# One Strassen pair for the down projections of the first two chunks, and a second layer norm moved into the gate/up blocks

## The chip, the cores and the metric

The kernel runs on one core of a Trainium2 chip. TensorE multiplies matrices into PSUM; VectorE (DVE), ScalarE (ACT) and GpSimd (POOL) work element by element; SyncE (SP) issues most DMA transfers, and each engine has its own instruction queue, worked off in order. The metric is the time of one execution on the device, in microseconds (us); lower is better. A profile is one such execution recorded instruction by instruction.

## What is computed

A transformer block over S = 2048 tokens of width 1024, in bf16:

```python
q, k, v = split(layernorm(x) @ wqkv)                 # 32 heads of 32
idx     = pos[:, None] - 2 * arange(8)[None, :]      # 8 earlier positions, dilation 2
attn    = softmax(where(idx >= 0, q . k[idx] / sqrt(32), -1e9))
h       = x + (attn . v[idx]) @ wo                   # wo: 1024 x 1024
g, u    = layernorm(h) @ w_gate, layernorm(h) @ w_up # 1024 x 3584 each
out     = h + (g * u) @ w_down                       # 3584 x 1024
```

## The kernel before

**Tiling.** The tokens are cut into four chunks of 512 (`TC`). For a chunk, the normalized activations lie transposed in a tile `lnT` (128 partitions x 8 x 512 columns; pool of three). A gate or up group is eight matmuls of 128x128 by 128x512 into one PSUM bank (`mm_group`, L409); the PSUM pool has eight banks, all of them under one tag. The product g*u of a chunk, transposed, is 28 cells of [128, 512], and the down projection contracts over those cells.

**Strassen.** Where the kernel says "pair", two halves of a matrix product are combined so that seven block products take the place of eight, on operands scaled and converted to f16, with sums and differences of blocks made on VectorE. The scales are powers of two from sums of absolute values: `Scale.add` (L553) takes them on ScalarE, one instruction with an accumulated sum and a short read of the accumulator, and `Scale.total` adds them over partitions with one matmul by ones.

**Order of the work on TensorE before.** The stages stand in the order in which the program calls them:

1. qkv of chunks 0 to 3, interleaved; output projection 0 with its norm (`wo_ln2(0)`, L519) lies amid the last qkv blocks;
2. `ffn1(0)` (L602): seven blocks of gate and up groups of chunk 0. ScalarE copies each bank out, VectorE multiplies g by u, and ScalarE takes the absolute sums of the gate weights (for chunk 1, in step 4, of the up weights and of its hidden cells);
3. `wo_ln2(1)`, then `ffn2(0)` (L640): chunk 0's down projection with plain matmuls, 2 halves x 28 cells x 4 row tiles = 224;
4. `ffn1(1)`, then chunk 1's down projection as a Strassen pair of its own: its four row tiles are split into two and two, `dprod` (L805) makes a product of one row tile by one block over 14 cells, and there are seven products for each of two row tiles. Output projections 2 and 3 (`wo_adds`, L846) lie between these products, with the sums and conversions as functions hung onto their groups;
5. the pair blocks: gate and up of chunks 2 and 3 as Strassen products (`pair_block`, L703), and the down projection of chunks 2 and 3 as one pair over four row tiles.

**Output projection and norm.** `wo_ln2` makes 8 groups (4 row tiles x 2 halves). VectorE adds each bank to the residual `hs[t]` (L534). When a row tile is whole, VectorE takes its statistics (L181, L182), ScalarE the inverse deviation (L185, L186), VectorE normalizes (L190), and SP issues a DMA transpose into `lnT2`. The next gate/up stage needs all four transposes of its `lnT2` at its first matmul.

**Attention** of a chunk is a generator of VectorE steps (2.3 us and less each) with loads and stores on POOL's queue. `Background` (L38 and on) slips one step of it, or of a norm, between two matmul groups: each group gives `GROUP_US` = 1.73 of credit times `bg.rate`, and each step, or `bg.spend`, uses some of it. `bg.finish(gen)` emits all that is left of a generator at once. This is done while the program is built, so that it sets the order of each engine's instructions and takes no time itself.

**Weights.** The list `stream` holds the weight blocks in the order of their use; `pump` (L161) issues the next loads on SP's queue into a pool `wpool` of seven buffers, and `retire` (L173) gives buffers back. A load waits, on SP, for the readers of the buffer it overwrites.

Of the kernel before, what the change touches and what calls it, by code (L numbers as in the profile page):

```python
# [18 lines left out]
D = 1024  # L19
# [59 lines left out]
def kernel(  # L79
# [41 lines left out]

    bg = Background()
# [13 lines left out]
    def stream_wd(c, hf):  # L136
        for b in range(4):
            stream.append((("wd", c, hf, b), wd_v[:, bass.ts(b, 7), bass.ts(hf, 512)], 7))

    NH = NF // 4  # L140
    for c in range(2):
        stream_wo(c)
        if c > 0:
            stream_wd(0, 0)
            stream_wd(0, 1)
        for b in range(7):
            stream.append((("wg", c, b), wg_v[:, :, bass.ts(b, 512)], KO))
            stream.append((("wu", c, b), wu_v[:, :, bass.ts(b, 512)], KO))
    def stream_down(name, e, hf, halves):
        for a in halves:  # L150
            stream.append((("dn", name, a), wd_e[e][:, bass.ts(a, 7), bass.ts(hf, 512)], 7))

    stream_down("21", 1, 0, (0, 1))
    stream_down("11", 0, 0, (0, 1))
    stream_wo(2)
    stream_down("12", 0, 1, (0,))
# [100 lines left out]
    class NormOnScalar(Norm1):  # L257

        def sums(self):
            room = small.tile([128, 4, 4], F32, tag="nroom", name=f"nroom{self.c}")  # L260
            self.s, self.nm, self.ss, self.nb = (room[:, i, :] for i in range(4))
            junk = lnp.tile([128, D], BF, tag="ln", name=f"njunk{self.c}")
            xs = xtiles[self.c]
            for t in range(4):
                nc.scalar.activation(junk[:], xs[t][:], ACTF.Copy, accum_out=self.s[:, t:t + 1])
                yield "later", GROUP_US
            nc.scalar.activation(self.nm, self.s, ACTF.Copy, scale=-1.0 / D)
            for t in range(4):
                nc.scalar.activation(junk[:], xs[t][:], ACTF.Square, bias=self.nm[:, t:t + 1],
                                     accum_out=self.ss[:, t:t + 1])  # L270
                yield "later", GROUP_US
# [4 lines left out]

        def rows(self):
            for t in range(4):
                ln = lnp.tile([128, D], BF, tag="ln", name=f"ln{self.c}_{t}")
                nc.scalar.activation(ln[:], xtiles[self.c][t][:], ACTF.Identity, bias=self.nb[:, t:t + 1],  # L280
                                     scale=self.rs4[:, t:t + 1])
                self.lns[t] = ln
                self.transpose(t)
                yield "later", GROUP_US
# [158 lines left out]

    def attention(c):
        qD, kD = qkv_in["q", c], qkv_in["k", c]
        lg = att.tile([128, W, SUB], F32, tag="lg", name=f"lg{c}")
        for wp in range(W // 2):
# [14 lines left out]
            yield 1.0  # L462
        if c == 0:
            nc.vector.tensor_tensor(lg[0:32, :, 0:16], lg[0:32, :, 0:16], mask[:], ALU.add)
# [54 lines left out]
    def wo_ln2(c):  # L519
# [8 lines left out]
        for t in range(4):  # L528
            for hf in range(2):
# [12 lines left out]
                bg.spend(0.7)  # L542
                bg.step(GROUP_US)
        norm(3)
        retire(2)
        return lnT, hs
# [35 lines left out]
    scale_gu, scale_d, scale_h = Scale("gu", 56), Scale("d", 56), Scale("h", 56)  # L582
    scale_h1 = Scale("h1", 28)

    def abs_sum(c, b, j):
        wt = wts["wg" if c == 0 else "wu", c, b]
        junk = lnp.tile([128, 2, 512], BF, tag="ln", name=f"junk{c}_{b}_{j}")
        scale_gu.add(28 * c + 4 * b + j, wt[:, bass.ts(j, 2), :], junk[:])

    def abs_sum_down(hf, b, j):  # L590
        junk = lnp.tile([128, 512], BF, tag="ln", name=f"junkd{hf}_{b}_{j}")
        scale_d.add(28 * hf + 7 * b + j, wts["wd", 0, hf, b][:, j, :], junk[:])
# [5 lines left out]
    def abs_sum_h1(f, ht):  # L598
        junk = lnp.tile([128, TC], BF, tag="ln", name=f"junke{f}")
        scale_h1.add(f, ht[:], junk[:])  # L600

    def ffn1(c, lnT, at={}):  # L602
        hT = []
        for b in range(7):
            if b == 5 and c + 1 < NCH:
                hss[c + 1] = load_x(c + 1, "h", nc.sync)
            for j in range(4):
                pg = psum.tile([128, TC], F32, tag="mm", name=f"pg{c}_{b}_{j}")
                mm_group(pg, wts["wg", c, b], j, lnT)
                gs = t1k.tile([128, TC], BF, tag="t1k", name=f"gs{c}_{b}_{j}")  # L610
                nc.scalar.copy(gs[:], pg[:])  # L611
                bg.step(GROUP_US)
                pu = psum.tile([128, TC], F32, tag="mm", name=f"pu{c}_{b}_{j}")
                mm_group(pu, wts["wu", c, b], j, lnT)
                us = t1k.tile([128, TC], BF, tag="t1k", name=f"us{c}_{b}_{j}")
                nc.scalar.copy(us[:], pu[:])  # L616
                nc.vector.tensor_tensor(gs[:], gs[:], us[:], ALU.mult)  # L617
                abs_sum(c, b, j)
                bg.spend(0.45)
                bg.step(GROUP_US)  # L620
                hT.append(gs)
                if (b, j) in at:
                    at[b, j]()
                f = len(hT) - 3
                if c == 1 and f >= 0:
                    abs_sum_h1(f, hT[f])
# [3 lines left out]
        if c == 1:  # L630
            for f in range(NF - 2, NF):
                abs_sum_h1(f, hT[f])
        return hT

    def ffn2_store(c, t, hf, acc, hs, lo=0, n=512):
        cols = bass.ds(hf * 512 + lo, n)
        nc.vector.tensor_tensor(hs[t][:, cols], acc[:], hs[t][:, cols], ALU.add)
        nc.sync.dma_start(outf[bass.ds(c * TC + t * 128, 128), cols], hs[t][:, cols])

    def ffn2(c, hf, hT, hs, between={}):  # L640
        acc = [psum.tile([128, 512], F32, tag="mm", name=f"acc{c}_{hf}_{t}") for t in range(4)]
        for b in range(4):
            for j in range(7):
                f = b * 7 + j
                for t in range(4):
                    nc.tensor.matmul(acc[t][:], lhsT=hT[f][:, bass.ts(t, 128)],  # L646
                                     rhs=wts["wd", c, hf, b][:, j, :],
                                     start=(f == 0), stop=(f == NF - 1))
                if c == 0:
                    abs_sum_down(hf, b, j)  # L650
                bg.step(0.86)
            retire()
            if b in between:
                between[b]()
        for t in range(4):
            ffn2_store(c, t, hf, acc[t], hs)
            bg.spend(0.7)


# [103 lines left out]
    start_attention(1)  # L763
    pump(pair_at)
# [3 lines left out]
    qkv(3, range(4), last=True)  # L768
    bg.finish(atts[0])
    bg.rate = 0.98  # L770
# [3 lines left out]
    lnT2, hs = nxt  # L774
    hT = ffn1(0, lnT2)
    bg.finish(atts[1])
    nxt = wo_ln2(1)
    for hf in range(2):
        ffn2(0, hf, hT, hs)
    lnT2, hs = nxt  # L780
# [37 lines left out]
    dn = {}  # L818

    def first_blocks():  # L820
        dn["11"] = [wts["dn", "11", a] for a in range(2)]
        dn["21"] = [wts["dn", "21", a] for a in range(2)]
        conv_down(dn["11"])

    hT = ffn1(1, lnT2, {0: scale_d.rows, 2: scale_d.total, (6, 1): first_blocks})
# [332 lines left out]
```

## Time and profile before

| What | us |
|---|---|
| median of 3 runs (lowest, highest) | 778.18 (777.26, 778.30) |
| the profiled execution: time | 777.01 |
| the profiled execution: span of the profile | 775.2 |
| `wo_ln2(0)` | 163.56 to 177.38 |
| `ffn1(0)` | 191.19 to 287.88 |
| `wo_ln2(1)` | 287.88 to 301.69 |
| `ffn2(0)` | 301.69 to 350.04 |
| `ffn1(1)` | 350.04 to 446.76 |
| chunk 1's down projection, projections 2 and 3 | 446.76 to 516.77 |
| pair blocks of chunks 2 and 3 | 516.77 to 687 |
| down projection of chunks 2 and 3 | 687 to 775 |

The stages are read off TensorE's timeline, by the first matmul of each. Busy time on an engine is the union of its instructions' durations. A duration can be longer than the distance to the next start, since neighbouring instructions on an engine overlap; where an engine is backed up, the distance between starts is what one more instruction costs. A releaser, written `<-`, is what ended a wait, as inferred from semaphores. Within a group line of the page, the fields are: line of the program, engine, operation, output<-input, shapes, count, busy us, mean ns of one, idle time just before.

### The profile page before, as it was taken

To read this page: it belongs to the slowest core of one execution; us is meant where nothing else is said; L and a number is where in the kernel's file an instruction comes from. 1 tells how busy PE (TensorE), PEld (TensorE's weight loads), DVE (VectorE), ACT (ScalarE), POOL (GpSimd) and SP (SyncE) were. 2 spreads that over 40 slices of the span, in tenths; PEclk is the share of its full clock that TensorE was granted. 3 is DMA by queue.
4 is the path that set the end of the run, shared out by engine and by line. 5 is a ranking of instruction groups with operands and counts; after the bars stand their busy time and mean duration, and the time that the engine had idled before them with its cause. 6 is when DMAs were issued, how large, how long until landed. Compare 5 with 4: busy or idle time off the path is not lost.

```text
span 775.2 us, 10420 instructions
## 1 busy us (share of the span) xinstructions
PE 769.3 (99%) x3691; PEld 353.5 (46%) x3691; DVE 605.3 (78%) x766; ACT 484.0 (62%) x1040; POOL 142.1 (18%) x152
## 2 busy tenths in 40 slices
PE   8999999999999999999999999999999999999998
PEld 6444444444444444444444444444444444444444
DVE  5639999999999989999979859985553444578863
ACT  4639564322866662965777899746677776788240
POOL 0000000200002000011000001008778687600000
PEclk9999999999999999999999999999999999999999
DMA  8998896997947964978445592644332423740001
GB/s 278 265 260 199 157 230 151 299 271 224 310 133 236 308 235 125 288 257 277 142 143 192 182 299 68 157 98 114 109 95 69 109 59 106 240 140 28 0 28 55
DMA packets 183716, 134.38 MB, mean 173 GB/s; under 512 B 81264, under 2 KB 176496, under 8 KB 181616
## 3 DMA queue, kind: packets, MB, share of 16 engines
q1 hardware_dynamic: 176912, 110.12, 50.9%
q0 software_dynamic: 3584, 22.02, 8.9%
q10 hardware_dynamic: 3168, 1.57, 0.8%
q8 instruction: 29, 0.48, 0.3%
q14 instruction: 23, 0.19, 0.1%
HBM read 104.86 MB, written 22.02 MB: 164 GB/s over the span
## 4 chain that ended last, share of the span: by engine, by line
PE 93%; DVE 3%; DMA 2%; ACT 1%; issue 0%; ACTq 0%; DVEq 0%
PE ps L411 20%; PE pg L411 12%; PE pu L411 12%; PE dx L807 6%; PE pz L700 6%; PE acc L646 6%; PE py L700 6%; PE px L700 6%; PE wo L532 4%; PE wo L852 4%; PE pv L700 3%; PE dy L807 3%; PE ex L807 2%; DMA lnT<-lnr 1%; DMA w_qkv<-in_A_wqkv_dram 1%; PE ps L372 1%
## 5 line engine op out<-in xcount | busy, mean ns | idle before, releaser
L411 PE MATMUL ps<-lnT,w_qkv 128*128 128x512 bf16 x736 | 159.5, 379 | 0.0
L411 PEld LDWEIGHTS <-w_qkv 128*128 128x128 bf16 x736 | 71.9, 98 | 86.2
L411 PE MATMUL pu<-lnT,w_wu 128*128 128x512 bf16 x448 | 105.8, 379 | 0.0
L411 PE MATMUL pg<-lnT,w_wg 128*128 128x512 bf16 x448 | 105.8, 379 | 0.0
L324 ACT CAST sg<-ps 128x512 bf16<-128x512 f32 x96 | 55.2, 585 | 52.3 <-PE ps L411 49.2
L451 DVE TENSOR_TENSOR prod<-qD,kD 128x4096 bf16<-128x4096 bf16 x32 | 72.4, 2285 | 12.8 <-DMA kD<-kd 12.7
L494 DVE TENSOR_TENSOR pv<-vD,at 128x4096 bf16<-128x4096 bf16 x32 | 72.5, 2285 | 0.3
L700 PEld LDWEIGHTS <-sw 128*128 128x128 f16 x448 | 43.8, 98 | 53.8 <-issue 1.2
L411 PEld LDWEIGHTS <-w_wu 128*128 128x128 bf16 x448 | 43.8, 98 | 52.9
L411 PEld LDWEIGHTS <-w_wg 128*128 128x128 bf16 x448 | 43.7, 98 | 52.8
L616 ACT CAST us<-pu 128x512 bf16<-128x512 f32 x56 | 33.0, 590 | 43.0 <-PE pu L411 41.8
L700 PE MATMUL px<-lnT,ws 128*128 128x512 bf16 x224 | 55.2, 379 | 0.0
L700 PEld LDWEIGHTS <-ws 128*128 128x128 f16 x336 | 32.9, 98 | 39.7
L506 POOL DMA_DIRECT2D od<-oD x4 | 2.2, 542 | 264.3 <-DVE oD L504 264.3
L646 PE MATMUL acc<-w_wd,gs 128*128 128x512 bf16 x224 | 48.5, 379 | 0.0
L681 POOL TENSOR_TENSOR sw<-ws 128x512 f16<-128x512 f16 x26 | 30.0, 1152 | 85.1 <-PE py L700 77.8
L611 ACT CAST gs<-pg 128x512 bf16<-128x512 f32 x56 | 32.6, 583 | 12.9 <-PE pg L411 10.6
L453 DVE TENSOR_TENSOR prod<-prod 128x4096 bf16<-128x4096 bf16 x16 | 36.6, 2289 | 0.4
L560 ACT ACTIVATE junkd<-w_wd 128x512 bf16<-128x512 bf16 x56 | 34.3, 613 | 0.0
L646 PEld LDWEIGHTS <-gs 128*128 128x128 bf16 x224 | 21.9, 98 | 26.4
L617 DVE TENSOR_TENSOR gs<-gs,us 128x512 bf16<-128x512 bf16 x56 | 23.5, 419 | 12.5 <-ACT us L616 12.5
L185 ACT ACTIVATE rs<-mv,eps 128x1 f32<-128x1 f32 (+1 forms) x21 | 6.2, 297 | 42.0 <-DVE mv L182 36.6
(321 smaller groups left out, 1391.5 us busy)
## 6 DMA issues: line engine op xcount, KB each, us to landing
w_wg<-in_B_w_gate_dram SPq DMA_DIRECT2D x14, 1024.0 KB, 6.7
w_wu<-in_B_w_up_dram SPq DMA_DIRECT2D x14, 1024.0 KB, 5.4
w_wd<-in_B_w_down_dram SPq DMA_DIRECT2D x8, 896.0 KB, 6.2
w_pair<-in_B_w_gate_dram SPq DMA_DIRECT2D x14, 512.0 KB, 4.0
w_pair<-in_B_w_up_dram SPq DMA_DIRECT2D x14, 512.0 KB, 5.2
w_wo<-in_A_wo_dram SPq DMA_DIRECT2D x6, 1024.0 KB, 6.2
w_qkv<-in_A_wqkv_dram SPq DMA_DIRECT2D x5, 1024.0 KB, 11.0
kd<-sg SPq DMA_DIRECT2D x32, 144.0 KB, 3.3
```

The lines of the kernel that those rows point to most:

```text
L324: nc.scalar.copy(sg[:, HB:HB + TC], ps[:])
L411: nc.tensor.matmul(ps[:], lhsT=wt[:, ko, bass.ts(j, 128)], rhs=rhs[:, ko, :], start=(ko == 0), stop=(ko == KO - 1))
L451: nc.vector.tensor_tensor(prod[:, j], qD[:], kD[:, :, o:o + SUB], ALU.mult)
L453: nc.vector.tensor_tensor(prod[:, :, 0:16], prod[:, :, 0:16], prod[:, :, 16:32], ALU.add)
L494: nc.vector.tensor_tensor(pv[:, j], vD[:, :, o:o + SUB], at[:, w, None, :].to_broadcast((128, DH, SUB)), ALU.mult)
L532: nc.tensor.matmul(ps[:], lhsT=oTs[c][:, kk, t, :], rhs=wts["wo", c, hf][:, kk, :], start=(kk == 0), stop=(kk == KO - 1))
L560: nc.scalar.activation(junk, src, ACTF.Abs, accum_out=self.l1[:, k:k + 1])
L611: nc.scalar.copy(gs[:], pg[:])
L616: nc.scalar.copy(us[:], pu[:])
L646: nc.tensor.matmul(acc[t][:], lhsT=hT[f][:, bass.ts(t, 128)], rhs=wts["wd", c, hf, b][:, j, :], start=(f == 0), stop=(f == NF - 1))
L700: nc.tensor.matmul(ps[:], lhsT=lhs[:, ko, :], rhs=rhs[:, ko, :], start=(fresh and ko == 0), stop=(ko == 3), skip_group_check=not fresh)
L807: nc.tensor.matmul(ps[:, bass.ds(lo, n)], lhsT=lhs[k][:, bass.ts(q, 128)], rhs=rhs[k][:, bass.ds(lo, n)], start=(fresh and k == 0), stop=( ...
```

## The change

**Chunk 0's plain down projection is gone.** `ffn2` is removed. Chunk 0's hidden cells stay in SBUF, chunk 1's are stored to DRAM (`hd1`) in pairs from a ring of small tiles, and reloaded. After both gate/up stages, chunks 0 and 1 are down-projected as one Strassen pair over four row tiles: 7 products x 4 row tiles x 14 cells.

**Output projection 1** moves from after `ffn1(0)` to before block 5 of chunk 0's gate/up (`ffn1_first`, called with `{5: wo_1}`). Its norm's row sums, squares and normalized rows are ScalarE activations (`Norm2`, a subclass of the norm that the qkv stage uses); the squares and rows are slipped into blocks 5 and 6 as a background generator.

**What goes with it.** Residual rows of chunks 0 and 1 are stored to DRAM (`hsd0`, `hsd1`) and reloaded into weight buffers. The absolute sums of w_down are taken earlier: blocks 0 to 2 are loaded on ScalarE's queue during qkv of chunks 2 and 3 (`abs_early`), blocks 3 to 7 during chunk 1's gate/up (`abs_gen`). Absolute sums of weights are 2048 wide instead of 1024 (gate and up) or 1024 instead of 512 (w_down). `bg.rate` goes from 0.98 to 1.0.

```diff
-    for c in range(2):
-        stream_wo(c)
-        if c > 0:
-            stream_wd(0, 0)
-            stream_wd(0, 1)
-        for b in range(7):
-            stream.append((("wg", c, b), wg_v[:, :, bass.ts(b, 512)], KO))
-            stream.append((("wu", c, b), wu_v[:, :, bass.ts(b, 512)], KO))
...
+    stream_wo(0)
+    for b in range(7):
+        if b == 5:
+            stream_wo(1)
+        stream_gu(0, b)
+    stream_wd(3)
+    stream_wd(4)
+    for b in range(7):
+        stream_gu(1, b)
+        if b < 3:
+            stream_wd(5 + b)
+    stream_down("11", 0, 0)
+    stream_down("21", 1, 0)
     stream_wo(2)
...
+    class Norm2(NormOnScalar):
...
+        def finish(self):
+            yield from self.devs()
+            yield from self.rows()
+            for t in range(4):
+                rows = hsd[self.c][:, t, :]
+                nc.sync.dma_start(rows, hss[self.c][t][:, D - rows.shape[-1]:D])
+
+    def wo_norm(c):
+        n = Norm2(c)
...
+                nc.vector.tensor_tensor(hs[t][:, bass.ts(hf, 512)], ps[:], hs[t][:, bass.ts(hf, 512)], ALU.add)
+                bg.spend(0.7)
+                if hf == 0 and t > 0:
+                    n.sum(t - 1)
+                bg.step(GROUP_US)
+        n.sum(3)
+        retire(2)
+        return n
...
+    def abs_early(blocks):
+        wt = wpool.tile([128, KO, 512], BF, tag="w", name="w_early")
+        state["live"] += 1
+        for i in blocks:
+            wts["wd", i] = wt
+            nc.scalar.dma_start(wt[:, 0:7, :], wd_block(i))
+            yield "later", 12.0
+            for k in range(4):
+                abs_sum_down(i, k)
+                yield "later", GROUP_US
+        retire()
...
+    def ffn1_first(lnT, at):
...
+            if b in at:
+                at[b]()
             for j in range(4):
...
+                if j % 2:
+                    abs_sum("wg", b, j // 2, junk[:])
+                sum_h(len(hT) - 2)
...
+    def ffn1_second(lnT, at):
+        ring = [lnTp.tile([128, KO, TC], BF, tag="lnT", name=f"ring{i}") for i in range(2)]
...
+        def finish():
+            i, g, u = late.pop(0)
+            nc.vector.tensor_tensor(g, g, u, ALU.mult)
+            bg.spend(0.75)
+            scale_h1.add(NF + i, g, junk[:, 0:2, :])
+            nc.sync.dma_start(hd1[:, bass.ts(i, 2), :], g)
...
-    bg.rate = 0.98
+    bg.finish(sums)
+    bg.finish(atts[0])
+    bg.rate = 1.0
     nxt = wo_ln2(0)
...
-    hT = ffn1(0, lnT2)
-    bg.finish(atts[1])
-    nxt = wo_ln2(1)
-    for hf in range(2):
-        ffn2(0, hf, hT, hs)
...
+    def wo_1():
+        bg.finish(atts[1])
+        n = wo_norm(1)
+        norm2.append(n)
+        norm2.append(n.finish())
+        bg.add(norm2[1], bg.now, first=True)
+
+    hT0 = ffn1_first(nxt[0], {5: wo_1})
+    bg.finish(norm2[1])
+    sums = abs_gen(range(3, 8), 0.0)
+    bg.add(sums, bg.now, first=True)
+    ffn1_second(norm2[0].lnT, {4: lambda: bg.finish(sums)})
...
+    load_down(b12, 0, 1)
...
+    load_h1(a21, 0)
+    load_h1(a22, 1)
...
+    for q in range(4):
+        dprod(xs[q], q, A11, cells_of(b11, NH), True)
...
+    for t, n in ((a21[0], 8), (a22[0], 8), (a21[1], 6), (a22[1], 6)):
+        to_f16(f16(t[:, 0:n, :]), t[:, 0:n, :], sh1, nc.scalar)
+    for q in range(4):
+        dprod(xs[q], q, A12, cells_of(b21, NH), False)
+        put(0, q, 0, hs0[q][:, 0:512], xs[q], 1.0, hs0[q][:, 0:512])
...
+    wo_adds(2, {0: in_turn(lambda: s1_half(0), lambda: conv_a(A11, F11, 0, 5)),
+                1: in_turn(lambda: s1_half(1), b22_homes, lambda: conv_a(A11, F11, 5, 10)),
+                2: in_turn(lambda: t_half(b11, b12, b11, 0), lambda: conv_a(A11, F11, 10, 14)),
+                3: lambda: t_half(b11, b12, b11, 1), 4: lambda: conv_a(A12, F12, 0, 5),
+                5: lambda: conv_a(A12, F12, 5, 10), 6: lambda: conv_a(A12, F12, 10, 14)})
...
+    for q in range(4):
+        ev = psum.tile([128, TC], F32, tag="mm", name=f"ev{q}")
+        dprod(ev, q, FS1, fcells(b11), True)
+        p = lnp.tile([128, TC], F32, tag="ln", name=f"ep5_{q}")
+        nc.scalar.activation(p[:], ev[:], ACTF.Copy, scale=inv1)
+        p5t.append(p)
+        if q < 2:
+            conv_down([b22[q]], nc.scalar)
+        s_sums(F11, FS1, F11, ALU.subtract, (0, 4, 8, 14)[q], (4, 8, 14, 14)[q])
+        if q >= 2:
+            t_half(t2, b22, b11, q - 2)
...
+    for q in range(4):
+        dprod(ys[q], q, F11, fcells(t2), False)
+        z = psum.tile([128, TC], F32, tag="mm", name=f"ez{q}")
+        nc.scalar.copy(z[:], ys[q][:])
...
+        dprod(ys[q], q, F12, fcells(b22), False)
...
+    wo_adds(3, {0: in_turn(lambda: scale_gu.total(psum.tile([128, TC], F32, tag="mm", name="l1psgu")), lambda: ln_means(2)), 1: lambda: conv_down([b21[0]], nc.scalar),
+                2: in_turn(lambda: ln_devs(2), lambda: conv_a22(0)), 3: lambda: conv_a22(1),
+                4: lambda: s_sums(F11, F22, F11, ALU.subtract, 0, 7),
+                5: in_turn(lambda: ln_stat(3, 0), lambda: ln_act_bias(2)),
+                6: in_turn(lambda: ln_stat(3, 1), lambda: s_sums(F11, F22, F11, ALU.subtract, 7, 14)),
                 7: lambda: ln_stat(3, 2)})
...
+        dprod(zs[q], q, F11, fcells(b12), False)
...
+        dprod(zs[q], q, F22, fcells(t4), False)
```

The products of the new pair come in this order: A11·b11, A12·b21, projection 2, FS1·b11 (FS1 = a21 + a22; b11 by then holds b12 - b11), F11·t2 (F11 by then holds FS1 - F11, t2 = b22 - b11), F12·b22, projection 3, F11·b12 (with b12 = b22 - b12), F22·t4. Capital F is chunk data converted to f16; the a's are chunk 1's reloaded pairs, the b's quarters of w_down.

## What was predicted, before the changed kernel was run

> **What bounds the kernel now.** I read the busy shares and the chain of waits first, then busy time by stage, the gaps in TensorE's timeline, then durations on ScalarE and landing times of transfers.
>
> ```profile
> PE 769.3 (99%) x3691; PEld 353.5 (46%) x3691; DVE 605.3 (78%) x766; ACT 484.0 (62%) x1040; POOL 142.1 (18%) x152
> PE 93%; DVE 3%; DMA 2%; ACT 1%; issue 0%; ACTq 0%; DVEq 0%
> L646 PE MATMUL acc<-w_wd,gs 128*128 128x512 bf16 x224 | 48.5, 379 | 0.0
> ```
> ```profile
> 191.19:287.88 96.69, 96.69 (x449) 43.81 (x448) 91.52 (x83) 62.61 (x117) 5.70 (x8) 1.00 0.78 249
> 287.88:301.69 13.81, 13.81 (x66) 6.27 (x64) 13.53 (x23) 3.70 (x10) 0.00 (x0) 1.00 0.52 154
> 301.69:350.04 48.35, 48.35 (x226) 21.90 (x224) 47.20 (x34) 35.30 (x116) 3.16 (x4) 1.00 0.78 241
> 446.76:521.19 74.43, 73.79 (x343) 33.29 (x341) 64.34 (x147) 58.99 (x80) 3.56 (x4) 1.00 0.58 156
> ```
> ```profile
> 519.08 1.02 PE L700 MATMUL pv<-prodx,sw 128*128 128x512 f16 x4 [0.41 <-DVE h L812]
> 521.19 1.02 PE L700 MATMUL pv<-prodx,sw 128*128 128x512 f16 x4 [0.22 <-DVE h L812]
> ```
>
> TensorE works 99% of the span at full clock. The stages (window, length, then busy PE, PEld, DVE, ACT, POOL, clock, DMA share, GB/s) are chunk 0's gate/up, output projection 1, chunk 0's plain down projection, and chunk 1's down projection. In the third, 224 matmuls take 48.35 us: 215.9 ns each, 1.727 us for a group of 8. The only gaps in mid-kernel are 0.41 and 0.22 us. So every matmul removed is worth 0.216 us, and every late operand costs its whole lateness. VectorE has 5 us free in 97 in the first stage and almost nothing in the next two; ScalarE has slack, but it is about to be asked for more.
>
> **The Trainium skill.** "TensorE: Matmul & The Clock Gate", section "Wait — 56ns, not 53.3ns?", gives 215.7 ns between warm matmuls of 512 columns; the trace has 215.9. "DMA: Bandwidth & Descriptors", section "Issuing engines are not separate DMA queues", says that queues share the same 16 engines: a load put on ScalarE's queue gets no bandwidth of its own. The trace agrees in kind: from 140 to 180 us, with SP and POOL both transferring, the share is 0.99 to 1.06 at 289 to 321 GB/s. For ScalarE see below.
>
> **Removed from TensorE.** Before: 224 matmuls of chunk 0's down projection and, for chunk 1 alone, 2 row tiles x 7 products x 14 = 196, together 420. After: 4 x 7 x 14 = 392. That is 28 fewer; the scale totals go from 2 wide + 2 narrow (64 columns, about 0.027 us) to 4 wide. Net -26 x 0.2159 - 2 x 0.027 = **-5.67 us**. The two gaps (0.63) belong to the old start of the pair blocks and may vanish: at best **-6.3**. This is all there is to gain; the rest is what TensorE may newly wait for.
>
> **Step 1: output projection 1 amid blocks 4 and 5, its norm on ScalarE.** Before, it ran at 287.88 to 301.69, and chunk 0's down projection (48 us) lay between it and ffn1(1), which needs lnT2_1. After, only blocks 5 and 6 do: projection at 260.25 (191.19 + 5 x 13.81) to 274.06, blocks 5 and 6 until 301.69, where ffn1_second's first matmul needs all four transposes. The chain:
>
> (a) attention 1 must now be finished by 260, so VectorE, in order, carries its rest and the eight evictions in one run. From the row it has reached at 255.5 to the last eviction are 22.4 us of rows (2.2 per 4096-element product, 0.60 per eviction, and so on): 277.9, 3.8 us after TensorE is done. The fourth row sum on ScalarE then ends at about 279.0.
>
> (b) ScalarE's order, from the compiled program, then puts these ahead of the end of the last normalized row:
>
> ```profile
> L560 ACT ACTIVATE junkd<-w_wd 128x512 bf16<-128x512 bf16 x56 | 34.3, 613 | 0.0
> L560 ACT ACTIVATE junk<-w_wg 128x1024 bf16<-128x1024 bf16 x28 | 29.9, 1067 | 0.0
> L877 ACT ACTIVATE lnjunk<-h,lnroom 128x1024 bf16<-128x1024 bf16 x4 | 4.6, 1148 | 1.1 <-DVE lnroom L875 1.0
> L889 ACT ACTIVATE lnr<-h,lnroom,rs 128x1024 bf16<-128x1024 bf16 x8 | 9.6, 1236 | 2.4 <-DVE lnroom L884 1.5 <-DMA lnT<-lnr 0.8
> L786 ACT ACTIVATE gs<-gs,sbh 128x512 f16<-128x512 bf16 x14 | 8.7, 711 | 0.0
> L786 ACT ACTIVATE w_dn<-w_dn,sbd 128x3584 f16<-128x3584 bf16 x2 | 6.4, 3268 | 0.0
> ```
> ```profile
> 400.40 0.60 ACT L616 CAST us<-pu 128x512 bf16<-128x512 f32 x1
> 400.87 1.08 ACT L560 ACTIVATE junk<-w_wu 128x1024 bf16<-128x1024 bf16 x1
> 401.83 0.22 ACT L560 ACTIVATION_READ_ACCUMULATOR junk<-w_wu 128x1 f32 x1
> 401.92 0.65 ACT L560 ACTIVATE junke<-gs 128x512 bf16<-128x512 bf16 x1
> ```
>
> Durations overlap, so the start-to-start times of a backlogged ScalarE count: 0.47 a copy, 0.96 + 0.09 an absolute sum of 1024, 0.52 + 0.09 of 512. A sum of 2048 is not in the trace; by the slope (0.44 per 512) it is 1.84 + 0.09 = 1.93. The skill's "ScalarE: Activation LUTs", section "What ACT_TABLE_LOAD costs", states 186 ns + 0.833 per element, 93 ns overlapped: 1.89 with the read, an estimate. (It fits the trace's 613 at 512; at 1024 it gives 1039, measured 1067.) I take 1.93. The list: 12 copies 5.64, 6 sums of hidden cells 3.66, 3 gate-weight sums 5.79, dependent pairs +0.36, 4 squares 4.6, attention's exponential 0.97, logarithm, exponential and biases 1.7, 4 rows 4.56: **27.3 us**. From 279.0: 306.3.
>
> (c) The last transpose:
>
> ```profile
> lnT<-ln SPq DMA_TRANSPOSE x16, 3.5
> ox<-in_B_w_down_dram SPq DMA_DIRECT2D x1, 896.0 KB, 11.8
> lx<-in_B_w_down_dram SPq DMA_DIRECT2D x1, 896.0 KB, 12.5
> ```
>
> Landings run from 3.0 to 3.5 after issue; with 3.2, lnT2_1 is there at 309.5. TensorE, in order, has only matmuls of this projection behind the waiting one: **+7.8 us**. Bounds: with no lag on VectorE 4.9 (ScalarE's first copy waits for 274.06 + 1.73 anyway); with more lag or slower transposes 9.7. The stall lets ScalarE and VectorE catch up, which helps later but pays nothing back.
>
> **Step 2: gate/up of chunk 1 with stores to DRAM.** Copies, sums of hidden pairs, up-weights and w_down give ScalarE 13.4 us of 13.81 per block in five blocks. Behind a late copy lie eight PSUM banks (seven groups, 12 us), which hide it: cost 0; if that cover were gone, 1 to 3. Chunk 0's residual goes out on SP behind its transposes; nobody waits for it until the end. This stage ends at E = 398.4 + 7.8 = 406.2.
>
> **Step 3: the pair, from E.** A11·b11 with totals ends at +12.5, A12·b21 at +24.6, projection 2 at +38.4, FS1·b11 at +50.5 (a first stall of about 0.15). Then F11·t2 needs t2 = b22 - b11, and b22 is converted by ScalarE last in its queue: a21 and a22 (reloads of the hidden pairs), 28 cells of chunk 0, two p5 copies, two halves of b22.
>
> ```profile
> 448.00:455.00 7.00, 7.00 (x35) 3.16 (x33) 1.13 (x5) 7.00 (x10) 0.00 (x0) 1.00 0.91 310
> ```
>
> The reloads come behind a projection weight, b12 and each other on SP, 6.5 MB in all. In the old kernel 4.6 MB issued together took up to 12.5 us, with a stretch at 310 GB/s. At about 300 the second half of a22 lands at +21.8 (20 to 22.7 for 340 to 288 GB/s). ScalarE, waiting for each, ends the four conversions at +28.3, 28 cells x 0.63 at +45.9, then 0.6 + 3.17 + 0.6 + 3.17: b22's second half is ready at +53.5. VectorE's subtraction of 3584 (2.0 to 2.3) gives +55.8. The first product reaches that half seven matmuls after its start, +52.1: **+3.7**, bounds 0 (loads at +18, ScalarE never idle) and 5.
>
> In projection 3 VectorE has evictions 4.8, chain of the scale 1.0, a22 again 1.28 + 1.12, fourteen differences 4.8, statistics 2.8: 15.6 us from +80.3, and 1.6 of waiting for evictions' groups between. The last F11 cell is ready at +97.5; F11·b12, from +92.6, reaches its last cell at +95.4: **+2.2** (0.5 to 3). The following F22·t4 waits for b21's second half: **+0.4**. What is late next is the activation sums of chunks 2 and 3, due as the pair blocks start, with about 0 us in hand after these stalls.
>
> **Step 4: earlier.** w_down blocks 0 to 2 join a saturated stretch, and projection 0's weights lose buffers and are issued near 144 and 150; before, one of them took 14.3 us there, and they are needed at 163.56 and 165.3. I take **+0.3** (0 to 4).
>
> Sum: -5.67 - 0.63 + 7.8 + 0.15 + 3.7 + 2.2 + 0.4 + 0.3 = **+8.2 us**. On the profiled execution (777.01, span 775.2) that gives 785.2; the shown median, 778.18, is 1.2 above it, so 786.4.
>
> **Rivals.**
> 1. *ScalarE keeps up (faster).* Place: 279 to 302. If the first three rows' squares run while copies wait, and VectorE is not behind, the transposes land within 2.5 us of 301.7; then ScalarE also meets t2, and about 1.2 of stalls stay: 778.2 - 6.3 + 3.7 = 775.6. It decides once all stalls together fall below 6.3. For it: ScalarE is busy only 62% of the span. Against: 27 us must pass in the 23 left after the projection, an addition of measured rows.
> 2. *Only the first stall, at its low end (no change).* 4.9 + about 1 later against -6.3: 778. For: VectorE's lag is my walk of in-order rows. Against: VectorE shows 91.5 busy of 96.7 there.
> 3. *Transfers bound it as well.* Projection 0's weights late by 3, reloads at 288 GB/s or less, lnT2_1 at 9.5: 778.2 - 6.3 + 3 + 9.5 + 5 + 3 = 792.4. For: shares near 1 before 180 and 0.91 around 450. Against: weights on SP have mostly met their time.
> 4. *The change does not do what it says* is excluded for the count: the compiled program has 3663 matmuls.
>
> **How the numbers follow.** Forecast 0.58, rival 1 0.13, rival 2 0.07, rival 3 0.22. The forecast's own range, from the bounds above, is 781 to 790.5. The range reaches down into rivals 2 and 1 and up to rival 3: 776.5 to 794. About 0.2%, 1.6 us, is what a measurement here can tell from no change. Faster 0.13, same 0.07, slower 0.80.
>
> **What would show it.** Right: 3663 matmuls; one gap of 5 to 10 us before the first pwg1 matmul, released by a transpose of ln2_1; one of 2 to 5 us at ey (F11·t2) released by VectorE's subtraction; one of 1 to 3 us at ez (F11·b12). Wrong: that first gap under 3 us, or TensorE waiting in projection 0 or on ring copies, or gaps that sum to under 6 us.

## The result, and where 20 us went

The changed kernel takes 797.99 us (median of 4 runs, 794.56 to 798.76), the kernel before 777.72 in the same comparison: a ratio of 1.0253, 95% interval 1.0221 to 1.0285. It is slower, as forecast, but by 20.3 us instead of 8.2. Its profiled execution has a span of 796.4 us and a mean granted clock of 0.989, where the kernel before had 1.000. From the page of the changed kernel, busy time and the chain that ended last:

```profile
PE 770.2 (97%) x3663; PEld 351.6 (44%) x3663; DVE 607.1 (76%) x720; ACT 517.6 (65%) x991; POOL 141.9 (18%) x152
PE 45%; DVE 32%; ACT 9%; DMA 7%; issue 5%; SPq 1%; DVEq 0%; POOLq 0%; ACTq 0%
```

TensorE has 28 matmuls fewer and yet is busy 0.9 us longer. Its part of the chain has fallen from 93% to 45%: for long stretches something else decides. (Where a kernel had one or two runs far longer than its others, 794 us and more, the medians and ratios below leave them out.) The waits of TensorE say what (line, what was waited for, us in total, times, longest):

```profile
PE pwg L440 <- DMA lnT<-ln: 8.9, 1, 8.9
PE pwu L440 <- DMA w_wu<-in_B_w_up_dram: 4.2, 1, 4.2
PE ey L936 <- DVE t L929: 3.7, 2, 2.1
PE ps L440 <- DMA lnT<-ln: 2.4, 1, 2.4
PE ez L936 <- DVE gs L1100: 2.2, 1, 2.2
```

The first, third and fifth are the waits that the prediction names. The second is one that it put at nothing, the fourth one of another stage. A second loss shows only in TensorE's timeline, as groups of eight matmuls that take more than 1.89 us (`...` marks lines left out):

```profile
313.11 3.57 PE L440 MATMUL pwg<-lnT,w_wg 128*128 128x512 bf16 x8 [8.86 <-DMA lnT<-ln]
316.48 2.06 PE L440 MATMUL pwu<-lnT,w_wu 128*128 128x512 bf16 x8
318.37 1.89 PE L440 MATMUL pwg<-lnT,w_wg 128*128 128x512 bf16 x8
...
362.43 3.59 PE L440 MATMUL pwu<-lnT,w_wu 128*128 128x512 bf16 x8 [4.19 <-DMA w_wu<-in_B_w_up_dram]
365.82 2.98 PE L440 MATMUL pwg<-lnT,w_wg 128*128 128x512 bf16 x8
368.63 1.89 PE L440 MATMUL pwu<-lnT,w_wu 128*128 128x512 bf16 x8
```

Two groups should take 3.45 us. They take 5.26 after the first wait and 6.20 after the second: 1.8 and 2.75 us lost after the operands were there. The clock that TensorE was granted (window, length, busy PE, clock, DMA share, GB/s) fell to one half during each wait and stayed there for 3.7 and 5.6 us after the matmuls had begun again:

```profile
304.25:306.56 2.31, 0.00 (x0) 1.00 1.04 335
306.56:313.11 6.55, 0.00 (x0) 0.50 1.16 280
313.11:316.80 3.69, 3.69 (x9) 0.50 1.01 315
316.80:320.00 3.20, 3.20 (x16) 1.00 0.99 325
...
361.18:362.43 1.25, 0.00 (x0) 0.50 1.08 399
362.43:368.00 5.57, 5.57 (x14) 0.50 1.09 385
368.00:372.00 4.00, 4.00 (x20) 1.00 0.84 303
```

Half of 3.7 and of 5.6 us is about what was lost. The next table has the time between the first matmul of one stage and that of the next, by the starts in TensorE's timeline, which lie up to 0.2 us ahead of those in the table of the kernel before. The last column is an estimate without waits, from 1.727 us a group and 0.2159 us a matmul:

| Stage | before | changed | without waits |
|---|---|---|---|
| up to chunk 0's gate/up | 191.0 | 193.6 | 191.0 |
| chunk 0's gate/up, projection 1 | 110.5 | 119.5 | 110.5 |
| chunk 0's plain down projection | 48.4 | none | none |
| chunk 1's gate/up | 96.7 | 105.6 | 96.7 |
| pair and projections 2, 3 | 70.2 | 120.2 | 112.9 |
| from the pair blocks on | 258.4 | 257.5 | |

So there is +2.6 before the change's own stages, +9.0 at lnT2_1, +8.9 in chunk 1's gate/up (4.3 of it the wait for w_wu, counted between starts, and 4.55 slow matmuls) and +7.3 in the pair, against some -5.6 of removed matmuls and -0.9 after them, where the two gaps of the kernel before are gone. In sum that is 21.2, the difference of the spans.

### The profile page after: what moved, and what is told of

It is laid out like the page before. It is cut to its first block, busy times and chain, and to the rows that moved or that the text cites. A ratio compares the mean times of both kernels' runs of the same rounds, so it can differ in the third digit from the quotient of the medians.

```text
span 796.4 us, 10310 instructions
## 1 busy us (share of the span) xinstructions
PE 770.2 (97%) x3663; PEld 351.6 (44%) x3663; DVE 607.1 (76%) x720; ACT 517.6 (65%) x991; POOL 141.9 (18%) x152
## 4 chain that ended last, share of the span: by engine, by line
PE 45%; DVE 32%; ACT 9%; DMA 7%; issue 5%; SPq 1%; DVEq 0%; POOLq 0%; ACTq 0%
DVE prod L482 6%; PE dx L936 6%; PE px L817 6%; PE py L817 6%; PE pz L817 6%; DVE pv L526 5%; DVE prod L484 3%; PE pv L817 3%; PE ez L936 3%; PE ey L936 3%; PE pwu L440 3%; PE dy L936 3%; PE pwg L440 3%; PE ps L440 3%; DMA w_wu<-in_B_w_up_dram 2%
## 5 line engine op out<-in xcount | busy, mean ns | idle before, releaser
L440 PE MATMUL pwg<-lnT,w_wg 128*128 128x512 bf16 x224 | 55.7, 394 | 8.9 <-DMA lnT<-ln 8.9
L440 PE MATMUL pwu<-lnT,w_wu 128*128 128x512 bf16 x224 | 54.8, 389 | 4.2 <-DMA w_wu<-in_B_w_up_dram 4.2
L440 PE MATMUL pg<-lnT,w_wg 128*128 128x512 bf16 x224 | 52.9, 379 | 0.1
L440 PE MATMUL pu<-lnT,w_wu 128*128 128x512 bf16 x224 | 52.9, 379 | 0.0
L936 PEld LDWEIGHTS <-gs 128*128 128x128 f16 (+1 forms) x280 | 27.3, 98 | 40.3 <-issue 4.3
L798 POOL TENSOR_TENSOR sw<-ws 128x512 f16<-128x512 f16 x26 | 30.0, 1153 | 84.4 <-PE pv L817 51.0
L834 ACT COPY py<-px 128x512 f32<-128x512 f32 x28 | 16.0, 570 | 28.5 <-PE px L817 28.5
L799 POOL TENSOR_TENSOR sw<-sw,ws 128x512 f16<-128x512 f16 x26 | 30.0, 1152 | 2.0
L801 POOL TENSOR_TENSOR sw<-ws,sw 128x512 f16<-128x512 f16 x26 | 30.2, 1161 | 0.0
L800 POOL TENSOR_TENSOR sw<-ws 128x512 f16<-128x512 f16 x26 | 30.0, 1153 | 0.0
```

Source lines behind the costliest of these rows:

```text
L440: nc.tensor.matmul(ps[:], lhsT=wt[:, ko, bass.ts(j, 128)], rhs=rhs[:, ko, :], start=(ko == 0), stop=(ko == KO - 1))
L798: eng.tensor_tensor(sw[:, i, 0], a21, a22, ALU.add)
L799: eng.tensor_tensor(sw[:, i, 1], sw[:, i, 0], a11, ALU.subtract)
L800: eng.tensor_tensor(sw[:, i, 2], a11, a21, ALU.subtract)
L801: eng.tensor_tensor(sw[:, i, 3], a12, sw[:, i, 1], ALU.subtract)
L834: nc.scalar.copy(yb[i][:], xb[i][:])
```

## Experiments

Differences between runs start early: in their profiles, the kernels below begin chunk 0's gate/up anywhere from 190.6 to 195.3 us. Experiment 7 takes this up, and leaves its cause open. Where totals are blurred by this, the stages' lengths are compared; they and all waits are read from one profiled execution of each kernel. Some of the recorded expectations call kernels by names such as `e6_norm`; the name is given where its kernel comes in.

**1. ScalarE's sums out of the norm's way.**

```diff
+                if hf == 0:
+                    abs_sum("wg", 5 + t // 2, t % 2, n.junkw[:])
                 if hf == 0 and t > 0:
                     n.sum(t - 1)
...
-                if j % 2:
+                if j % 2 and b < 5:
```

> The four absolute sums of the gate weights of blocks 5 and 6 are moved on ScalarE from between the norm's squares and rows to output projection 1, where ScalarE waits for VectorE. Theory A (separate waits, each worth its own length, and TensorE at half clock for a while after a long one): the wait for lnT2_1 falls from 8.9 to about 3.1 us, the slow restart behind it (1.8 us) mostly goes, the wait for w_wu stays near 4; 790 to 792 us against the changed kernel's 798. Theory B (the transfers during chunk 1's gate/up are the bound, and the wait for lnT2_1 only hides it): what is saved comes back as a longer wait for w_wu, 8 to 11 us, and the time stays at 796 to 798.

Measured: 797.27 us, ratio 1.0262 (1.0239 to 1.0285). Neither theory: w_wu is waited for 4.3 us (4.2 before), so nothing came back there, but the wait at lnT2_1 is still 8.2. ScalarE's last row did end 3.1 us earlier, counted from the start of the stage. Something after ScalarE holds the transposes. In the changed kernel, ScalarE's rows and then SP's queue (start, duration, instruction) read:

```profile
299.84 1.24 ACT L305 ACTIVATE ln<-h,nroom,rs 128x1024 bf16<-128x1024 bf16 x1
...
304.15 1.92 ACT L635 ACTIVATE junk_g<-w_wg 128x2048 bf16<-128x2048 bf16 x1
...
306.82 1.23 ACT L305 ACTIVATE ln<-h,nroom,rs 128x1024 bf16<-128x1024 bf16 x1
```
```profile
299.49 1.24 SPq L560 DMA_TRANSPOSE lnT<-ln  x1
300.84 0.52 SPq L179 DMA_DIRECT2D w_wu<-in_B_w_up_dram  x1
301.40 0.57 SPq L179 DMA_DIRECT2D w_wd<-in_B_w_down_dram  x1
302.07 4.61 SPq L560 DMA_TRANSPOSE lnT<-ln  x1
306.77 2.85 SPq L560 DMA_TRANSPOSE lnT<-ln  x1
309.72 1.26 SPq L560 DMA_TRANSPOSE lnT<-ln  x1
```

Two weight loads stand between the first and the second transpose. They waited behind the first one, which waited for ScalarE, and went out only then (at 300.8 and 301.4; with the transposes behind them, in experiment 2, they go out at 290.4 and 297.9). The next three transposes then occupy SP for 8.9 us, where the first took 1.24. The last row is ready at 308.05, but its transpose is issued at 309.72.

**2. The same place from both sides.** Three kernels: SP's order alone (`e5_loads_first`), ScalarE's order alone (`e9_act_only`: experiment 1's edit, with the sums of the last eleven hidden cells also put behind the rows), and both (`e6_norm`, in whose text "the last kernel" is the one with SP's order alone). The main lines of the edits:

```diff
-            yield from self.rows()
+            for t in range(4):
+                self.row(t)
+                yield "later", GROUP_US
+            for t in range(4):
+                self.transpose(t)
...
-                sum_h(len(hT) - 2)
+                if b < 5:
+                    sum_h(len(hT) - 2)
+                else:
+                    left.append(len(hT) - 2)
```

> Only SP's order is changed: the four transposes of lnT2_1 stand behind the loads of w_wu_0 and w_down block 4 instead of around them, so that these loads no longer wait for ScalarE's first row and no longer move beside the transposes. Theory A (ScalarE's backlog is the bound of lnT2_1, the loads a second one close behind it): the last transpose is issued as ScalarE ends its row and lands 3 to 3.5 us later; the wait at lnT2_1 falls from 8.9 to 6 to 7.5 us, and w_wu of block 3, with its loads some 10 us earlier, waits under 2 us: 791 to 795 us. Rival (transfers during chunk 1's gate/up are the bound): w_wu waits as before, 4 us or more: 796 to 798.

> ScalarE's part of e6_norm alone: the sums of gate weights 5 and 6 in output projection 1, the last hidden cells' sums behind the rows, and SP's order left as in the changed kernel (two weight loads stuck between the first and second transpose). Two bounds in series: ScalarE's rows are done some 6 us earlier but SP still issues the transposes slowly beside the loads, so the wait at lnT2_1 stays at 4 to 8 us: 791 to 797 us. Rival (ScalarE's backlog was the only bound, and e1_sums_early merely moved too little of it): a wait of 2 us or less, 785 to 788 us.

> The last kernel's order on SP, and ScalarE's sums of gate weights 5 and 6 in output projection 1, and its sums of the last eleven hidden cells behind the normalized rows. Theory A (two bounds in series, ScalarE and SP, and only both together free lnT2_1): wait at lnT2_1 0 to 3 us with no slow restart, 785 to 790 us, or 4 more where w_wu then waits. Rival (VectorE's lag in output projection 1 is the bound): a wait of 5 us or more stays: 793 to 796.

| Kernel | median, us | ratio (95%) | wait at lnT2_1 | projection-1 stage |
|---|---|---|---|---|
| SP alone | 793.46 | 1.0225 (1.0181 to 1.0269) | 8.36 | 119.0 |
| ScalarE alone | 794.77 | 1.0220 (1.0186 to 1.0253) | 6.28 | 117.0 |
| both | 784.13 | 1.0097 (1.0074 to 1.0120) | 1.21 | 111.9 |

With SP's order alone, the last row on ScalarE and its transpose on SP (each from its engine's timeline) follow at once, and ScalarE decides:

```profile
308.46 1.23 ACT L305 ACTIVATE ln<-h,nroom,rs 128x1024 bf16<-128x1024 bf16 x1
```
```profile
309.71 1.23 SPq L560 DMA_TRANSPOSE lnT<-ln  x1
```

With ScalarE's order alone, the row is done at 300.5 and SP comes to its transpose 4.9 us later, so that SP decides:

```profile
299.29 1.25 ACT L305 ACTIVATE ln<-h,nroom,rs 128x1024 bf16<-128x1024 bf16 x1
```
```profile
305.41 1.26 SPq L560 DMA_TRANSPOSE lnT<-ln  x1
```

The two gains alone are 0.5 and 2.6 us of stage length; together they are 7.6. These are two limits in series, one hidden close behind the other. With both, chunk 1's gate/up falls as well, from 105.6 to 100.7: no clock drop follows the first wait, and w_wu is waited for 2.1 us. The forecast for SP alone (a wait of 6 to 7.5) was too hopeful: ScalarE's row came no earlier. Its four runs fall into two pairs, 789.8 and 790.3, 796.6 and 797.2; the profile is of the first. The forecast for ScalarE alone held; both together came out 0.9 us below the range given. The rival for "both", VectorE's lag as the limit, falls: it accounts for at most the 1.2 us left.

**3. Slow matmuls: a restart, or late operands?**

```diff
+        fill(36, hT0[0][:])
         for b in range(7):
...
+                    if (what, b, j) == ("wu", 3, 0):
+                        fill(16, hT0[0][:])
```

> TensorE gets matmuls whose result is not used: 36 in the wait for lnT2_1 (7.8 of its 8.9 us) and 16 in the wait for w_wu of block 3 (3.5 of its 4.2 us). If the slow matmuls behind these waits (0.43 us apart instead of 0.216) are TensorE restarting at half clock after idling, they run at full clock now and the time falls by 1.8 + 2.7 us at most, to 793.5, or to 795 if the landing of w_wu is fixed and takes the 1.8 back. If they are slow because operands come late, nothing changes: 797.5 to 798.5.

TensorE's timeline of this kernel, at the same two places:

```profile
315.27 1.89 PE L440 MATMUL pwg<-lnT,w_wg 128*128 128x512 bf16 x8 [2.65 <-DMA lnT<-ln]
...
363.90 1.90 PE L440 MATMUL pwu<-lnT,w_wu 128*128 128x512 bf16 x8 [1.86 <-DMA w_wu<-in_B_w_up_dram]
```

Both groups run at full speed, and the profiled clock is 1.000 again. So the slow matmuls were TensorE coming out of idling, not late operands. The time did not show it: 797.19 us, ratio 1.0255 (1.0215 to 1.0295), the expected fall missed. Chunk 1's gate/up did shorten, from 105.6 to 102.2: the 2.75 us are gone, but of the first 1.8 only 0.7 stayed, and 1.1 came back as a longer time until w_wu was there. In the rest of this run lnT2_1 landed 1.6 us later, counted from the start of its stage, and a new wait of 1.9 us stands at the start of the pair blocks; why is not shown.

**4. Why w_wu is late.** The kernel without the loads and sums of w_down blocks 3 to 7:

```diff
-    stream_wd(3)
-    stream_wd(4)
...
-    sums = abs_gen(range(3, 8), 0.0)
-    bg.add(sums, bg.now, first=True)
-    ffn1_second(norm2[0].lnT, {4: lambda: bg.finish(sums)})
+    ffn1_second(norm2[0].lnT, {})
```

> The loads of w_down blocks 3 to 7 and their absolute sums are left out, so that the scale of w_down comes from three of its eight blocks: 4.6 MB fewer transfers, fewer weight buffers held and 20 us less on ScalarE, nearly all during chunk 1's gate/up. Theory A: the wait for w_wu (4.2 us) and its slow restart (2.7) go, the wait for lnT2_1 stays at 8 to 9: 791 us. Rival: the attention's loads and stores alone crowd out w_wu: the wait stays over 3 us and the time at 796 to 798.

Measured 792.57 us, ratio 1.0188 (1.0167 to 1.0210): the wait is gone, and chunk 1's gate/up takes 98.4. In the changed kernel the load was issued at 345.3, needed at 358.1 and landed 17.1 us after its issue. It waited for ScalarE, and went out as ScalarE had done with an absolute sum over an earlier block of up weights and read the accumulator (first ScalarE's timeline, then SP's):

```profile
343.23 1.91 ACT L635 ACTIVATE ring<-w_wu 128x2048 bf16<-128x2048 bf16 x1
345.04 0.19 ACT L635 ACTIVATION_READ_ACCUMULATOR ring<-w_wu 128x1 f32 x1
```
```profile
345.26 0.86 SPq L179 DMA_DIRECT2D w_wu<-in_B_w_up_dram  x1
```

While it is under way, attention 2's store and loads on POOL's queue move as well. By windows of that kernel (clock, DMA share and GB/s last):

```profile
338.00:342.00 4.00, 4.00 (x20) 1.86 (x19) 3.97 (x3) 4.00 (x11) 0.54 (x1) 1.00 0.30 108
342.00:346.00 4.00, 4.00 (x21) 1.76 (x19) 3.29 (x3) 3.75 (x7) 0.00 (x0) 1.00 0.98 289
346.00:350.00 4.00, 4.00 (x20) 1.85 (x19) 3.77 (x3) 4.00 (x9) 3.06 (x4) 1.00 1.04 344
350.00:354.00 4.00, 4.00 (x21) 1.76 (x19) 3.63 (x5) 4.00 (x7) 1.02 (x2) 1.00 1.08 348
```

It looks like a collision, not a lack of bandwidth over the stage: just before it the share is 0.30. In the kernel with SP's order alone the load is issued at the same 345.4, attention's loads of oT start at 348.8 instead of 346.9, the load lands after 11.8 us, and no wait is left in the profiled run (98.2 for the stage). Without the w_down blocks it goes out 4.4 us earlier in the stage and lands after 7.7 us, although attention 2's transfers stay. Two quite different edits each remove the wait; the margin is a few us either way. Experiment 4 takes away transfers, ScalarE's work and held buffers at once, so which of them makes the load late is not shown.

**5. The pair's own waits.** ScalarE converts b22 ahead of chunk 0's odd cells, and VectorE makes the differences for F11·b12 ahead of the statistics:

```diff
+    conv_down(b22, nc.scalar)
...
-        if q < 2:
-            conv_down([b22[q]], nc.scalar)
+        conv_a(A12, F12, (0, 4, 8, 11)[q], (4, 8, 11, 14)[q])
...
-                5: in_turn(lambda: ln_stat(3, 0), lambda: ln_act_bias(2)),
+                5: in_turn(lambda: s_sums(F11, F22, F11, ALU.subtract, 7, 14), lambda: ln_act_bias(2)),
```

> On ScalarE b22 is converted ahead of chunk 0's odd cells, and on VectorE the differences for F11·b12 go ahead of two row tiles' statistics. Theory A: the waits at F11·t2 (3.7 us) and F11·b12 (2.2 us) go and nothing takes their place: 792 us. Rival: the next piece is late by as much (the odd cells' differences at F12·b22, or chunk 3's rows and the activation sums at the start of the pair blocks): 795 to 798 with a new wait of 2 us or more.

Measured 795.32 us, ratio 1.0222 (1.0192 to 1.0252), at the lower end of the rival's range. Both waits are gone, and waits of 1.08 and 1.72 us take their place at F22·t4, for VectorE's `b21r`: the rival was right in part. The stage fell from 120.2 to 116.0. With the differences for F22·t4 and the residual additions also ahead of the statistics, on top of experiment 2's "both", "the last kernel" of the next text (this one is `e7_all`):

> The last kernel with the conversions and differences of the pair reordered as before, and the differences for F22·t4 and the additions of chunk 1's residual ahead of the statistics. If the waits are separate and add up: 7 us less than the last kernel, no wait over 1 us at F11·t2, F11·b12 or F22·t4, 779 to 783 us. If they hide one another: a new wait of 2 us or more at F22·t4 or at the pair blocks: 784 to 788.

Measured 780.55 us, ratio 1.0047 (1.0031 to 1.0064). The pair stage falls from 119.8 to 113.6 and none of the three waits is over 1 us, so in the stage the waits do add up. Of the 6.2 us, 1.2 come back as a wait at the pair blocks; the total fell by 3.6, not by the 7 expected, though it lies in the forecast range.

**6. A version that closes the account.** On top of `e7_all`, w_down blocks 3 and 4 (`e10_spread`; in `e11_spread2` also one of the three early ones) are loaded and summed in chunk 0's gate/up:

```diff
-    stream_wd(3)
-    stream_wd(4)
+        if b in (0, 2):
+            stream_wd(3 + (0, 2).index(b))
...
-        if b < 3:
-            stream_wd(5 + b)
+        if b in (1, 2, 3):
+            stream_wd(5 + (1, 2, 3).index(b))
```

> e7_all with w_down blocks 3 and 4 loaded and summed during chunk 0's gate/up (blocks 0 to 4, where ScalarE has 3.7 us free per block) and blocks 5 to 7 one block later than before. If the wait for w_wu left in e6_norm and e7_all (2.2 us and 1.3 us of slow restart) comes from ScalarE's backlog and held buffers at the start of chunk 1's gate/up, it goes: 777 to 779 us. If the attention's loads and stores cause it, it stays: 781 to 782.

> e10_spread with one of the three early w_down blocks also moved from the qkv stage into chunk 0's gate/up. If the early blocks on ScalarE's queue delay output projection 0's weights, chunk 0's gate/up starts at 191 to 192.5 us instead of 193 to 195: 775 to 777 us. If not, as e10_spread, 777 to 779.

Measured 778.17 and 778.16 us, ratios 1.0009 (0.9999 to 1.0020) and 1.0011 (1.0000 to 1.0023): w_wu no longer waits, and chunk 1's gate/up takes its 96.7. Moving one early block gained nothing that can be seen. Next, on top of `e11_spread2`, fewer attention steps between projection 1's evictions, and two results written out ahead of the activation sums (`e13_best`):

```diff
+                if 2 * t + hf in (4, 5, 6):
+                    bg.spend(GROUP_US)
...
-    activation_sums(l2, l3, px)
     for q in range(4):
         dprod(zs[q], q, F22, fcells(t4), False)
+        if q == 2:
+            activation_sums(l2, l3, px)
```

> e11_spread2 with three attention steps fewer between the evictions of output projection 1 on VectorE, and with two results of F22·t4 written out ahead of the activation sums. If the 1.6 us wait at lnT2_1 is VectorE's lag and the 1.2 us wait at the pair blocks is a PSUM bank held behind the sums, both go: 775 to 776 us, faster than the kernel before. If what stays is set by the landing of transposes and attention moves the lag elsewhere: 777.5 to 778.5.

Measured 775.97 us, ratio 0.9986 (0.9977 to 0.9995). The profiled run took 772.77 us (span 770.9), the fastest of 22, and had none of the early waits; all the waits of TensorE after its first 9 us are these:

```profile
405.35 0.39 PE L654 MATMUL ey<-rowbh,ones 128*128 128x512 bf16 x1 [0.98 <-DVE rowbh L649]
412.18 12.25 PE L950 MATMUL ex<-w_dn,gs 128*128 128x512 bf16 x56 [0.40 <-DVE ey L999]
501.01 1.67 PE L950 MATMUL ez<-b21r,a22r 128*128 128x512 f16 x7 [0.17 <-DVE hsr L785]
502.94 10.74 PE L950 MATMUL ez<-b21r,a22r 128*128 128x512 f16 x49 [0.26 <-DVE b21r L943]
```

They sum to 1.8 us, 1.2 more than before; with -5.67 for the matmuls this gives -4.5, and the spans differ by -4.3. The account closes for this execution; that the median lies 3.2 us above it is the subject of experiment 7.

**7. The waits ahead of chunk 0's gate/up.** Up to about 100 us both programs have the same instructions on every engine, yet the changed one and its variants often show waits near 40 us, and also near 102 and at projection 0. Three kernels: the early w_down loads left out of the changed kernel; the kernel before with the new DRAM buffers declared; the last version with all early blocks in chunk 0's gate/up.

> The changed kernel without the early loads and sums of w_down blocks 0 to 2 (the scale of w_down comes from five of its eight blocks): 2.8 MB fewer transfers on ScalarE's queue between 105 and 150 us. If these crowd out output projection 0's weights, the first gate group of chunk 0 starts within 0.5 us of 191.2 as in the kernel before (193.6 in the changed kernel) and the time falls by 2 to 3 us, to 795; if the waits before it come from something else, it starts at 192.5 to 195 as in the others, and the time stays at 797 to 798.

> The kernel before with the changed kernel's three DRAM buffers (hd1, hsd0, hsd1) declared and not used. Up to about 105 us the two programs have the same instructions on every engine, yet the changed kernel and its variants show waits of 0.4 to 2.4 us near 40 and 102 us that the kernel before does not show. If the placing of the DRAM buffers causes them, this kernel gets them too and takes 778.5 to 781 us; if not, 777.0 to 777.8, as the kernel before.

> e13_best with no w_down block loaded in the qkv stage: blocks 0 to 4 are loaded and summed on SP's stream during chunk 0's gate/up. If the early loads on ScalarE's queue cause the varying waits ahead of chunk 0's gate/up (0 to 4 us from run to run), the runs draw together at 772 to 774 us with a spread under 2 us. If not, the spread stays at 772 to 778 with a median near 776. If five more sums make ScalarE late in chunk 0's gate/up, a wait at lnT2_1 or at a weight block comes back: over 776.

Without the early loads, chunk 0's gate/up starts at 191.6, as forecast for that case, but the kernel takes 800.62 us, ratio 1.0301 (1.0286 to 1.0317), not 795. The start is 2.0 us earlier than in the changed kernel, lnT2_1 only 1.3; the waits at lnT2_1 and w_wu are 9.6 and 5.2 instead of 8.9 and 4.2, and the slow matmuls behind each cost 3.0 instead of 1.8 and 2.75. Why the later stages grow is not shown. Declaring the buffers does nothing: 777.09, ratio 1.0003 (0.9995 to 1.0011). The last version without early loads takes 774.72, ratio 0.9963 (0.9951 to 0.9975), the best of all, with runs from 773.1 to 777.3, between the two forecasts; its profile still waits 0.9 us near 102 us and 1.6 at 193.8. So it is about 1.3 us faster than the version with two early blocks, but the early loads are not what makes the runs vary; with all three of them, the kernel of experiment 5's first edit shows no early wait in its profile and starts at 191.0. That cause stays open.

## Why the prediction was right in direction and wrong in size

- **Removed from TensorE, -5.67**: right. The last versions, with nearly all waits gone, show it.
- **Step 1, +7.8**: measured +9.0. The walk along VectorE and ScalarE holds: the last row was predicted to end at 306.3 and ended at 308.05, in a stage that began 2.6 us later than before. The price for a sum of 2048, 1.84 + 0.09 between starts, was 1.81 + 0.23. What failed is (c): "landings run from 3.0 to 3.5 after issue" took the transpose as issued when its row is ready. SP, with two weight loads and two slow transposes in front, issued it 1.7 us later; from issue to landing the four took 2.7, 9.2, 5.4 and 3.3 us. The prediction left out what the moved step queues behind on SP. In the changed kernel this is a small error, but it is why mending ScalarE alone gives so little.
- **Step 2, "cost 0"**: the step that failed most. It reckoned cover in PSUM banks and ScalarE's time for copies, and put nothing on the weight loads, whose buffers and queue ScalarE's work also holds up. Measured: 4.3 us of wait for w_wu and 2.75 of restart. The new loads and stores of this stage were never laid beside attention 2's transfers, which come in one burst; how much of the delay is theirs stays open (experiment 4).
- **A term left out**: the slow matmuls after an idle stretch, 4.55 us in all. The Trainium skill, "TensorE: Matmul & The Clock Gate", section "What's actually happening", states that the array drops to half its clock after an idle window of about 3.4 us and needs about as long to recover. The trace agrees in the length: every half-clock stretch inside these runs lasts 3.41 us or two or three times that. The prediction used the page for the warm interval only. Its wait of 7.8 us should have carried the restart as well: the twelve waits of 4.0 to 9.6 us in all the traces were followed by losses of 1.5 to 3.0 us.
- **Step 3**: F11·t2 +3.7, measured 1.65 + 2.08, a wait for each half of t2; F11·b12 +2.2, measured 2.24 and 0.7 more, as its next seven matmuls follow VectorE's differences 0.335 us apart at full clock; F22·t4 +0.4, measured no wait. The order of conversions as cause is shown by experiment 5, and so is what the prediction called late next: once these go, F22·t4 and the pair blocks wait.
- **Step 4, +0.3 (0 to 4)**: measured 2.6, within its bounds, but by luck: 2.36 of it is a wait for transposes at 41 us, before the first of the moved loads.

In sum, the profiled execution was predicted to take 785.2 us and took 798.3. Of the missing 13 us, 4.55 are the restart, 4.3 w_wu, 2.3 the early stretch, 1.2 step 1 and the rest mostly the slow matmuls of F11·b12. Rival 3 named a cause of the right kind, transfers, and its 9.5 us at lnT2_1 came close to the 9.0 measured, but it put the rest at projection 0's weights and the reloads, not at w_wu.

## What to carry to other kernels

A wait is not only its own length: here every wait of TensorE over 4 us brought 1.5 to 3.0 us of slow matmuls with it, and some of 2.1 to 2.4 us did. When a step that ends in DMAs is moved, write down what stands before and after these DMAs in their issuing queue; a DMA that waits for a slow engine holds the loads behind it (here two, issued 10.4 and 3.5 us later than with the transposes behind them), and they then went out right among the transposes. And before a late operand is mended, look for the second limit close behind the first: either alone gained 0.5 and 2.6 us here, both 7.6.

## What was not expected of the hardware

Waits shorter than 3.4 us can cost the clock, too. In the kernel with both mends the wait before a matmul group was 2.11 us, and this group and the next took 5.15 us instead of 3.45. The clock fell only after the matmuls had begun again, for 3.41 us:

```profile
350.61 3.09 PE L440 MATMUL pwu<-lnT,w_wu 128*128 128x512 bf16 x8 [2.11 <-DMA w_wu<-in_B_w_up_dram]
353.49 2.43 PE L440 MATMUL pwg<-lnT,w_wg 128*128 128x512 bf16 x8
355.76 1.89 PE L440 MATMUL pwu<-lnT,w_wu 128*128 128x512 bf16 x8
```
```profile
350.60:351.17 0.57, 0.56 (x3) 1.00 1.08 390
351.17:354.58 3.41, 3.41 (x10) 0.50 1.04 383
354.58:358.00 3.42, 3.42 (x17) 1.00 1.04 378
```

In the kernel without w_down blocks 3 to 7, waits of 2.35 and 2.07 us were followed by a granted clock of 0.56 and 0.53; in the changed kernel, waits of 2.36 and 2.08 us were not (1.00). So the same length may or may not cost it: of the twenty waits of 2.0 to 2.7 us in all the traces, five were followed by half clock, and after the first 9 us none of the shorter ones was. And issuing a transpose took 1.24 us of SP's time for the first one in the changed kernel and 4.6 for the second, directly behind two weight loads; in `e13_best` the second of four took 4.68, directly behind another transpose. What makes it long is not shown.
